# Evictions, operand builds and one held-back product of a three-stage attention and gated-layer kernel: where they stand and which engine runs them

## The chip, the cores and the metric

The kernel runs on one core of a Trainium2 chip. The metric is the device time of one execution in microseconds (us). The profiler times every instruction of one execution. The core has five instruction streams that run beside each other, each in its own order: PE (TensorE, the matrix engine), ACT (ScalarE), DVE (VectorE), POOL (GpSimd) and SP (SyncE), which here issues the DMA transfers.

## The reference

```python
def reference(q, k, v, moe_*, moe2_*):
    # attention: 4 x 8 heads, 576 tokens, head size 64; keys and values averaged over 8 tokens
    attn = softmax(q @ k_p.T / 8) @ v_p            # (4, 8, 576, 64)
    x = attn.transpose(0, 2, 1, 3).reshape(2304, 512)
    # first gated layer, 512 -> 1536 -> 512
    xn = x / sqrt(mean(x * x) + 1e-6) * rms_g
    g = xn @ w_gate
    x = (g * sigmoid(g) * (xn @ w_val)) @ w_out
    # second gated layer, 512 -> 1536 -> 512
    return ((x @ w_a) * (x @ w_b)) @ w_out2        # (2304, 512)
```

The weights of both layers arrive as 64-bit floating point numbers and are converted on the chip.

## The kernel before, in words

**Precision.** Every large matmul is done as three: an operand t is split into a high part (a copy rounded to the type fp32r, made by ScalarE) and a low part (t minus the high part, a subtraction on VectorE or GpSimd). The product is then low x high + high x high + high x low, summed in PSUM, the matrix engine's result memory of 8 banks.

**First layer.** The 2304 tokens are worked off in five tiles of 512, 256, 512, 512 and 512. For each of 12 weight blocks of 128 columns, the loop at the end of the kernel function issues the products g and v (`project`), SiLU, the multiply of both (L1228, VectorE, which frees the PSUM bank of v), the split of the result (L1231, L1232) and, one block later, the output product into four accumulators (`out_proj`). `split_w` (L618) splits the weights of the next block, the low part on GpSimd (L622). After the last block the four accumulators are evicted (L1242): copies 0 and 2 on ScalarE, 1 and 3 on VectorE, into tiles `ev` of the pool `ev_p`, which has two buffers, and stored to DRAM (`x2d`) by SP.

**Second layer.** The tokens are taken in three blocks s of 768, each cut in two halves of tokens and two halves of the 512 features. `w_a` and `w_b` are treated as one 2 x 2 block matrix, and the 2 x 2 block product is computed in Winograd's form with seven block products instead of eight. `build(s, ...)` (L842) prepares the token side: it loads the four quarters, forms the differences t1 to t4 in place (`less`, L874, VectorE) and splits the seven operands b00, b10, t1, b11, t2, t3, t4 (`cast`, L863, ScalarE; `low`, L868: the first feature half on VectorE, the second on GpSimd, two instructions each). It returns eleven steps. `combine` and `convert` do the like for the weight side.

`group(f, s, side)` (L1026) issues six of the seven products of weight block f and token block s, each of six matmuls with 384 columns, into three banks X, Y and Z: X with b00, Y with t1, Z with b10, then further terms on top: X with t2, Y with b11, X with t3. Between them stand copies out of the banks on ScalarE (`snap`, L1023: p1, p5, u2) and additions on VectorE (L1043, L1049, L1054, L1055). After each product one entry of the list `side` is issued (`beside`), and so the build's steps are spread over the groups. The seventh product (t4, on top of X) of a group is held back and issued by `flush` (L1060) in the middle of the next group; it can start only when VectorE's L1054 has read X.

Build 0 runs beside the last tile of the first layer, in `second_front`, one step per quarter of a weight block. Build 1 runs in groups (0, 0) and (1, 0), build 2 in (0, 1) and (1, 1); then come (0, 2), (1, 2) and all others. The pools of the second layer take over the memory of the first's; an instruction that writes into such memory waits until the tile that lay there has been read or stored.

**Output projection.** `out_block` (L1106) adds, for each s, the products of the 12 hidden blocks into six accumulators; `prepare` loads and splits the weights (L1084, L1085) and hidden values (L1093, L1094) of the blocks ahead.

**Order.** In the last tile and the second layer the order of the instructions of PE, ACT, DVE and POOL is that of the program (`manual_schedule`). SP's order is chosen when the kernel is compiled. An engine whose next instruction waits does nothing else.

Of the kernel before, what the change touches and what calls it, by code (L numbers as in the profile page):

```python
# [8 lines left out]
F32 = mybir.dt.float32  # L9
# [8 lines left out]
P = 128  # L18
UNIT = 256
TILES1 = [512, 256, 512, 512, 512]  # L20
SLICE = 768
# [34 lines left out]
def starts(sizes):  # L56
    out, t = [], 0
    for n in sizes:
        out.append((t, n))
        t += n  # L60
    return out
# [3 lines left out]
def attention_moe_moe2(  # L65
# [14 lines left out]
    nc = tc.nc  # L80
# [7 lines left out]
    KD = DM // P  # L88
# [17 lines left out]
    x_p = first.enter_context(tc.tile_pool(name="x", bufs=1))  # L106
    h_p = first.enter_context(tc.tile_pool(name="h", bufs=2))
    ev_p = first.enter_context(tc.tile_pool(name="ev", bufs=2))
# [729 lines left out]
    two = {}  # L838
# [3 lines left out]
    def build(s, new, quarter):  # L842

        part = {}

        def load(h):
            t0 = s * SLICE + h * HALF
            for k in range(2):
                part[h, k] = quarter(f"x_{s}_{h}_{k}")
                for s0, sn in starts(TILES1):  # L850
                    lo, hi = max(s0, t0), min(s0 + sn, t0 + HALF)
                    if lo < hi:
                        for c in range(2):
                            row = (2 * k + c) * P
                            nc.sync.dma_start(
                                out=part[h, k][c][:, lo - t0:hi - t0],
                                in_=x2d[s0][row:row + P, lo - s0:hi - s0],
                            )

        def cast(i, h, k):  # L860
            hi, lo = XC[s, i] = new(s, i)
            for c in range(2):
                nc.scalar.copy(hi[:, c], part[h, k][c])  # L863

        def low(i, h, k):
            hi, lo = XC[s, i]
            for c in range(2):
                (nc.vector if c == 0 else nc.gpsimd).tensor_sub(  # L868
                    lo[:, c], part[h, k][c], hi[:, c].bitcast(F32)
                )  # L870

        def less(dst, a, b):
            for c in range(2):
                nc.vector.tensor_sub(part[dst][c], part[a][c], part[b][c])  # L874

        loads = [lambda: load(0), lambda: load(1)]
        return loads, [
            lambda: (cast("b00", 0, 0), cast("b10", 0, 1)),
            lambda: (low("b00", 0, 0), low("b10", 0, 1)),
            lambda: less((0, 0), (1, 0), (0, 0)),  # L880
            lambda: (cast("t1", 0, 0), cast("b11", 1, 1)),
            lambda: (low("t1", 0, 0), low("b11", 1, 1)),
            lambda: less((0, 0), (1, 1), (0, 0)),
            lambda: (cast("t2", 0, 0), less((1, 0), (1, 1), (1, 0))),
            lambda: (low("t2", 0, 0), cast("t3", 1, 0)),
            lambda: (less((0, 1), (0, 1), (0, 0)), low("t3", 1, 0)),
            lambda: cast("t4", 0, 1),
            lambda: low("t4", 0, 1),
        ]
# [116 lines left out]
    def bank(name):  # L1006
        return two["ps"].tile([P, 512], F32, tag="bank", name=name, bufs=8)

    def product(dst, f, a, s, b, start, stop):
        wh, wl, c0 = WC[f, a]  # L1010
        xh, xl = XC[s, b]
        i = 0
        for c in range(2):
            for w, x in ((wl, xh), (wh, xh), (wh, xl)):
                nc.tensor.matmul(  # L1015
                    dst[:, :HALF], w[:, c0 + c, :], x[:, c, :],
                    start=(start and i == 0), stop=(stop and i == 5), skip_group_check=True,
                )
                i += 1
# [40 lines left out]
    def flush():  # L1060
        if not pending:
            return
        f, s, X, c00 = pending.pop()
        product(X, f, A11, s, "t4", False, True)
        nc.vector.tensor_mul(c00, c00, X[:, :HALF])
        store(f, s, 0, c00)
# [3 lines left out]
    def store(f, s, h, src):  # L1070
        if (f, s) not in hd:
            hd[f, s] = dr.tile([P, SLICE], F32, tag=f"h_{f}_{s}", name=f"h_{f}_{s}")
        nc.sync.dma_start(out=hd[f, s][:, h * HALF:(h + 1) * HALF], in_=src)
# [25 lines left out]
    def prepare():  # L1099
        if todo:  # L1100
            s, f = todo.pop(0)
            if s == 0:
                out_weights(f)
            hidden_of(s, f)

    def out_block(s):  # L1106
        accs = [bank(f"o_{s}_{i}") for i in range(SLICE // P)]

        def add(f, i):
            wh, wl = WO[f]  # L1110
            hh, hl = HO[s, f]
            sub = slice(i * P, (i + 1) * P)
            for j, (x, y) in enumerate(((hh, wl), (hh, wh), (hl, wh))):
                nc.tensor.matmul(  # L1114
                    accs[i], x[:, sub], y, start=(f == 0 and j == 0), stop=(f == NF - 1 and j == 2),
                )

        for f in range(NF - 2):
            for i in range(len(accs)):
                add(f, i)  # L1120
            prepare()
        prepare()
        for i, acc in enumerate(accs):
            for f in range(NF - 2, NF):
                add(f, i)
            ev = two["o"].tile([P, 512], F32, tag="ev2", name=f"ev_{s}_{i}", bufs=3)
            if i % 2 == 0:
                nc.scalar.copy(ev, acc)
            else:
                nc.vector.tensor_copy(ev, acc)  # L1130
            t0 = s * SLICE + i * P
            nc.sync.dma_start(out=out[t0:t0 + P, :], in_=ev)
        prepare()

    later = ctx.enter_context(ExitStack())

    def second_phase():
        def pool(name, **kw):
            return tc.tile_pool(name=name, bufs=1, reuse_waits="tile", **kw)

        two["ps"] = ctx.enter_context(pool("ps2", space=bass.MemoryType.PSUM))
        two["w"] = later.enter_context(pool("w2", side="right"))
        bottom, middle = ctx.enter_context(ExitStack()), ExitStack()
        two["q"] = bottom.enter_context(pool("q2"))
        two["x2"] = bottom.enter_context(pool("x2"))
        two["x1"] = middle.enter_context(pool("x1"))

        def new(s, i):
            return [
                two[f"x{s}"].tile([P, 2, HALF], F32R, tag=f"{i}{e}", name=f"x{e}_{i}_{s}", bufs=1)  # L1150
                for e in "hl"
            ]

        def quarter(name):
            t = two["q"].tile([P, 2, HALF], F32, tag="xq", name=name, bufs=4)
            return [t[:, c] for c in range(2)]

        idle = [lambda: None]
        loads, steps = build(1, new, quarter)
        group(0, 0, loads + idle + steps[:4])  # L1160
        group(1, 0, steps[4:])
        loads, steps = build(2, new, quarter)
        group(0, 1, loads + idle + steps[:4])
        group(1, 1, steps[4:])
        group(0, 2, convert(2, 0) + convert(2, 1))
        group(1, 2, combine(2))
        for f in range(2, NF):
            group(f, 0, convert(f + 1, 0) + convert(f + 1, 1) if f + 1 < NF else convert(NF - 3, 2) + convert(NF - 2, 2))
            group(f, 1, combine(f + 1) if f + 1 < NF else convert(NF - 1, 2))
            if f < NF - 1:  # L1170
                group(f, 2, convert(f - 2, 2))
        middle.close()
        two["o"] = ctx.enter_context(pool("o2"))
        group(NF - 1, 2, idle + [prepare] + idle * 2 + [prepare])
        flush()
        later.close()
        two["r"] = ctx.enter_context(pool("o3", side="right"))
        for s in range(NS2):
            out_block(s)

    last_act = [None]
    for idx, (ph, t0, n) in enumerate(work):
        last_tile = idx + 1 == len(work)
        nxt = None if last_tile else work[idx + 1]
        side = SIDE[idx] if idx < len(SIDE) else []
        region = ExitStack()
        if last_tile:
            attn.close()
            side = second_front()
# [6 lines left out]
        def step():  # L1196
# [6 lines left out]
        accs = first_tile() if idx == 0 else [  # L1203
            ps.tile([P, 512], F32, tag=f"acc{c}", name=f"acc{c}") for c in range(KD)
        ]
# [3 lines left out]
        for f, cols, last, ahead, own in jobs:  # L1209
# [22 lines left out]
            low = nc.vector.tensor_sub(hl[:, :m], ht[:, :m], hh.bitcast(F32)[:, :m])  # L1232
# [7 lines left out]
        if nxt is not None:  # L1240
            xs = split_x(xf_t[idx + 1], nxt[2])
        for c, acc in enumerate(accs):  # L1242
            ev = ev_p.tile([P, 512], F32, tag="ev", name="ev")
            if c % 2 == 0:
                nc.scalar.copy(ev[:, :n], acc[:, :n])
            else:
                nc.vector.tensor_copy(ev[:, :n], acc[:, :n])
            nc.sync.dma_start(out=x2d[t0][c * P:(c + 1) * P, :], in_=ev[:, :n])
        region.close()
    first.close()  # L1250
    with tc.manual_schedule(engines=set(HELD)):
        second_phase()
# [36 lines left out]
```

## Time and profile before

| | |
|---|---|
| three runs | 1046.12, 1047.18, 1047.91 us (median 1047.18) |
| the profiled execution | 1046.91 us, of which the span from the first to the last instruction is 1045.0 |
| PE busy | 978.8 us, 94% of the span |
| DVE, ACT, POOL busy | 63%, 46%, 43% |
| mean granted clock of TensorE | 0.98 of full speed |

Busy shares are means over the whole span; where PE is not busy late in the kernel can be seen in a timeline. In the rows, a line of a timeline gives start, duration, engine, source line, operation and tiles, how many instructions were merged (x2), and in brackets the idle time before it with what ended it. "x<-ev" is a store of an evicted accumulator, "x<-x" a load of a token quarter. The first-layer part ends at about 611 us of the span, the groups at about 890.

### The profile page before, as it was taken

How to read it: one execution, taken by the hardware profiler on the slowest of the kernel's cores; microseconds unless marked ns; L12 is line 12 of the kernel's file. 1: busy time of each engine (PE TensorE's matmuls, PEld its weight loads, DVE VectorE, ACT ScalarE, POOL GpSimd, SP SyncE). 2: the span in 40 equal slices, each digit the busy share in tenths (PEclk: the TensorE clock that was granted, in tenths of full speed). 3: DMA queues.
4: the chain of work that ended last, by engine and by line, in shares of the span. 5: the costliest groups of instructions: out<-in, count | busy, mean ns of one | idle time of the engine just before them, and what ended most of it. 6: DMA issues, size and time to landing. Idle time of an engine off the chain costs nothing.

```text
span 1045.0 us, 13959 instructions
## 1 busy us (share of the span) xinstructions
PE 978.8 (94%) x5044; PEld 858.4 (82%) x5044; DVE 663.0 (63%) x992; ACT 477.0 (46%) x900; POOL 453.0 (43%) x360
## 2 busy tenths in 40 slices
PE   4977899889899999999999988999999998999998
PEld 3766677778788887888788878999999998888886
DVE  6999988996853756363627859766677665322221
ACT  3765764565454536444445435443444434222211
POOL 6476584646543434343359834533334332310000
PEclk9799899999899999999999999999999999999999
DMA  9456534330100002000111133434444444544332
GB/s 231 138 178 192 168 105 123 108 90 2 31 10 21 1 1 61 1 1 1 41 43 60 41 109 99 142 124 152 126 145 143 131 126 170 182 139 136 126 117 74
DMA packets 82804, 101.57 MB, mean 97 GB/s; under 512 B 24112, under 2 KB 63024, under 8 KB 82736
## 3 DMA queue, kind: packets, MB, share of 16 engines
q1 hardware_dynamic: 82736, 100.69, 31.3%
q8 instruction: 40, 0.66, 0.3%
q14 instruction: 28, 0.23, 0.1%
HBM read 73.93 MB, written 26.74 MB: 96 GB/s over the span
## 4 chain that ended last, share of the span: by engine, by line
PE 72%; DVE 18%; issue 3%; DMA 3%; ACT 2%; POOL 1%; SPq 1%; DVEq 0%; ACTq 0%; POOLq 0%
PE o L1114 14%; PE X L1015 13%; PE acc L663 9%; PE g L650 9%; PE v L650 9%; PE Y L1015 6%; PE Z L1015 3%; PE xT L400 2%; PE g L788 2%; DVE wf L600 2%; DVE kp L190 1%; PE sc L319 1%; PE v L788 1%; DVE wf L597 1%; DVE x L874 1%
## 5 line engine op out<-in xcount | busy, mean ns | idle before, releaser
L622 POOL TENSOR_TENSOR wl<-wf,wh 128x512 fp32r<-128x512 f32 x163 | 225.5, 1391 | 226.2 <-ACT wh L621 223.7
L621 ACT CAST wh<-wf 128x512 fp32r<-128x512 f32 x180 | 109.3, 619 | 72.6 <-PE acc L663 32.4
L663 PE MATMUL acc<-hh,wl 128*128 128x512 f32 (+1 forms) x248 | 92.2, 372 | 8.9 <-ACT hh L1231 5.7
L1094 DVE TENSOR_TENSOR hl<-hf,hh 128x768 fp32r<-128x768 f32 x36 | 35.6, 993 | 96.5 <-ACT hh L1093 96.5
L663 PE MATMUL acc<-hl,wh 128*128 128x512 f32 (+1 forms) x248 | 90.2, 368 | 3.6 <-DVE hl L806 3.4
L663 PE MATMUL acc<-hh,wh 128*128 128x512 f32 (+1 forms) x248 | 90.4, 365 | 0.0
L1114 PE MATMUL o<-woh,hl 128*128 128x512 f32 x216 | 86.0, 398 | 0.0
L1114 PE MATMUL o<-woh,hh 128*128 128x512 f32 x216 | 85.3, 395 | 0.0
L1114 PE MATMUL o<-wol,hh 128*128 128x512 f32 x216 | 84.9, 393 | 0.0
L650 PE MATMUL v<-xh,wl 128*128 128x512 f32 (+1 forms) x192 | 72.6, 378 | 2.8 <-DVE ht L1228 2.7
L1093 ACT CAST hh<-hf 128x768 fp32r<-128x768 f32 x36 | 29.8, 834 | 93.6 <-PE o L1114 87.0
L650 PE MATMUL g<-xh,wl 128*128 128x512 f32 (+1 forms) x192 | 71.4, 372 | 0.0
L650 PE MATMUL g<-xl,wh 128*128 128x512 f32 (+1 forms) x192 | 70.8, 369 | 0.1
L650 PE MATMUL g<-xh,wh 128*128 128x512 f32 (+1 forms) x192 | 70.9, 369 | 0.0
L650 PE MATMUL v<-xl,wh 128*128 128x512 f32 (+1 forms) x192 | 69.9, 364 | 0.0
L650 PE MATMUL v<-xh,wh 128*128 128x512 f32 (+1 forms) x192 | 69.6, 363 | 0.0
L607 POOL TENSOR_TENSOR wf<-wf,st 128x512 int32<-128x512 int32 x36 | 52.8, 1467 | 37.2 <-DVE wf L600 17.8
L607 POOL TENSOR_TENSOR w<-w,st 128x512 int32<-128x512 int32 x24 | 31.9, 1331 | 78.5 <-DVE w L600 77.3
L663 PEld LDWEIGHTS acc<-hh,wl 128*128 128x128 f32 x248 | 47.4, 191 | 17.5 <-issue 6.9
L1023 ACT COPY p<-X 128x384 f32<-128x384 f32 x36 | 17.2, 478 | 89.3 <-PE X L1015 89.3
L663 PEld LDWEIGHTS acc<-hl,wh 128*128 128x128 f32 x248 | 46.8, 191 | 12.8 <-DVE hl L806 4.5
L1228 DVE TENSOR_TENSOR ht<-ht,v 128x512 f32<-128x512 f32 (+1 forms) x48 | 29.6, 616 | 42.1 <-PE v L650 40.9
(208 smaller groups left out, 2782.7 us busy)
## 6 DMA issues: line engine op xcount, KB each, us to landing
hf<-h SPq DMA_DIRECT2D x36, 384.0 KB
st<-in_moe_w_out_dram SPq DMA_DIRECT2D x24, 512.0 KB
h<-u SPq DMA_DIRECT2D x36, 192.0 KB
h<-p SPq DMA_DIRECT2D x36, 192.0 KB
st<-in_moe_w_gate_dram SPq DMA_DIRECT2D x12, 512.0 KB
st<-in_moe_w_val_dram SPq DMA_DIRECT2D x12, 512.0 KB
st<-in_moe_w_a_dram SPq DMA_DIRECT2D x12, 512.0 KB
st<-in_moe_w_b_dram SPq DMA_DIRECT2D x12, 512.0 KB
```

The lines of the kernel that those rows point to most:

```text
L400: nc.tensor.matmul(bank[:, off:off + cnt], lhs, rhs, start=(i == 0), stop=(i == len(pairs) - 1),)
L607: nc.gpsimd.tensor_tensor(out=bits, in0=bits, in1=low, op=ALU.add)
L621: nc.scalar.copy(wh, wf[ph, f, i])
L622: (nc.vector if boot["alt"] else nc.gpsimd).tensor_sub(wl, wf[ph, f, i], wh.bitcast(F32))
L650: nc.tensor.matmul(bank[:, :n], w[:, c, :], x[:, c, cols], start=(i == 0), stop=(i == 3 * KD - 1),)
L663: nc.tensor.matmul(accs[c][:, cols], w[:, c, :], x[:, :n], start=(f == 0 and i == 0 and cols.start == 0), stop=(f == NF - 1 and i == 2),)
L788: nc.tensor.matmul(bank[:, :n], w[:, c, :], x[:, c, cols], start=(c == 0 and i == 0), stop=(c == KD - 1 and i == 2),)
L1015: nc.tensor.matmul(dst[:, :HALF], w[:, c0 + c, :], x[:, c, :], start=(start and i == 0), stop=(stop and i == 5), skip_group_check=True,)
L1093: nc.scalar.copy(hh, hf)
L1094: nc.vector.tensor_sub(hl, hf, hh.bitcast(F32))
L1114: nc.tensor.matmul(accs[i], x[:, sub], y, start=(f == 0 and j == 0), stop=(f == NF - 1 and j == 2),)
L1228: nc.vector.tensor_mul(ht[:, :m], ht[:, :m], vb[:, :m])
```

## The change

Three edits are made.
1. In the last tile the four evictions go into the four quarters of one tile of the pool `x_p` (the tag of the tile's input, which is no longer needed) instead of the two `ev` buffers.
2. In `build`, all low parts run on VectorE. The eleven steps are cut anew: one cast of an operand per step where there were up to two, each low part one step later than its cast.
3. The flush after the last group, with the closing of the pools that go with it, moves into the first output block (s = 0), behind the products of hidden block 0 with the first two of the six accumulators. Accumulators are therefore taken one by one, as they are first used.

```diff
@@ -865,9 +865,7 @@
         def low(i, h, k):
             hi, lo = XC[s, i]
             for c in range(2):
-                (nc.vector if c == 0 else nc.gpsimd).tensor_sub(
-                    lo[:, c], part[h, k][c], hi[:, c].bitcast(F32)
-                )
+                nc.vector.tensor_sub(lo[:, c], part[h, k][c], hi[:, c].bitcast(F32))
 
         def less(dst, a, b):
             for c in range(2):
@@ -875,14 +873,14 @@
 
         loads = [lambda: load(0), lambda: load(1)]
         return loads, [
-            lambda: (cast("b00", 0, 0), cast("b10", 0, 1)),
-            lambda: (low("b00", 0, 0), low("b10", 0, 1)),
-            lambda: less((0, 0), (1, 0), (0, 0)),
-            lambda: (cast("t1", 0, 0), cast("b11", 1, 1)),
-            lambda: (low("t1", 0, 0), low("b11", 1, 1)),
-            lambda: less((0, 0), (1, 1), (0, 0)),
+            lambda: cast("b00", 0, 0),
+            lambda: low("b00", 0, 0),
+            lambda: (less((0, 0), (1, 0), (0, 0)), cast("b10", 0, 1)),
+            lambda: (cast("t1", 0, 0), low("b10", 0, 1)),
+            lambda: (cast("b11", 1, 1), low("t1", 0, 0)),
+            lambda: (less((0, 0), (1, 1), (0, 0)), low("b11", 1, 1)),
             lambda: (cast("t2", 0, 0), less((1, 0), (1, 1), (1, 0))),
-            lambda: (low("t2", 0, 0), cast("t3", 1, 0)),
+            lambda: (cast("t3", 1, 0), low("t2", 0, 0)),
             lambda: (less((0, 1), (0, 1), (0, 0)), low("t3", 1, 0)),
             lambda: cast("t4", 0, 1),
             lambda: low("t4", 0, 1),
@@ -1104,9 +1102,11 @@
             hidden_of(s, f)
 
     def out_block(s):
-        accs = [bank(f"o_{s}_{i}") for i in range(SLICE // P)]
+        accs = []
 
         def add(f, i):
+            if f == 0:
+                accs.append(bank(f"o_{s}_{i}"))
             wh, wl = WO[f]
             hh, hl = HO[s, f]
             sub = slice(i * P, (i + 1) * P)
@@ -1115,9 +1115,16 @@
                     accs[i], x[:, sub], y, start=(f == 0 and j == 0), stop=(f == NF - 1 and j == 2),
                 )
 
+        NA = SLICE // P
         for f in range(NF - 2):
-            for i in range(len(accs)):
+            for i in range(NA):
                 add(f, i)
+                if f == 0 and s == 0 and i == 1:
+                    flush()
+                    later.close()
+                    two["r"] = ctx.enter_context(
+                        tc.tile_pool(name="o3", bufs=1, side="right", reuse_waits="tile")
+                    )
             prepare()
         prepare()
         for i, acc in enumerate(accs):
@@ -1172,9 +1179,6 @@
         middle.close()
         two["o"] = ctx.enter_context(pool("o2"))
         group(NF - 1, 2, idle + [prepare] + idle * 2 + [prepare])
-        flush()
-        later.close()
-        two["r"] = ctx.enter_context(pool("o3", side="right"))
         for s in range(NS2):
             out_block(s)
 
@@ -1240,7 +1244,12 @@
         if nxt is not None:
             xs = split_x(xf_t[idx + 1], nxt[2])
         for c, acc in enumerate(accs):
-            ev = ev_p.tile([P, 512], F32, tag="ev", name="ev")
+            if last_tile:
+                if c == 0:
+                    last_x = x_p.tile([P, KD, 512], F32, tag="xf", name="last_x")
+                ev = last_x[:, c]
+            else:
+                ev = ev_p.tile([P, 512], F32, tag="ev", name="ev")
             if c % 2 == 0:
                 nc.scalar.copy(ev[:, :n], acc[:, :n])
             else:
```

## Rows read from the trace of the kernel before

**Rows 1.** The profile's chain that ended last: shares of the span by engine.

```profile
PE 72%; DVE 18%; issue 3%; DMA 3%; ACT 2%; POOL 1%; SPq 1%; DVEq 0%; ACTq 0%; POOLq 0%
```

**Rows 2.** Timeline of PE at the start of the second layer.

```profile
610.75 0.34 PE L1015 MATMUL X<-xh_b,al 128*128 128x384 f32 x1
...
615.39 0.45 PE L1015 MATMUL Z<-xh_b,al 128*128 128x384 f32 x1 [2.39 <-ACT ev L1245]
...
620.34 0.33 PE L1015 MATMUL X<-xh_b,al 128*128 128x384 f32 x1
...
625.05 0.44 PE L1015 MATMUL X<-xh_t,sl 128*128 128x384 f32 x1 [1.43 <-ACT p L1023]
...
642.61 0.44 PE L1015 MATMUL X<-xh_t,sl 128*128 128x384 f32 x1 [1.46 <-ACT p L1023]
...
655.83 0.34 PE L1015 MATMUL X<-xh_b,al 128*128 128x384 f32 x1
...
663.11 0.34 PE L1015 MATMUL X<-xh_b,al 128*128 128x384 f32 x1
```

**Rows 3.** Timeline of ACT in the same stretch.

```profile
614.75 0.58 ACT L1245 COPY ev<-acc 128x512 f32<-128x512 f32 x1 [5.26 <-DMA x<-ev]
...
618.63 0.48 ACT L1023 COPY u<-X 128x384 f32<-128x384 f32 x1 [2.53 <-DMA x<-ev]
...
622.82 0.98 ACT L863 CAST xh_t<-x 128x384 fp32r<-128x384 f32 x2 [2.06 <-DVE x L874]
...
624.53 0.47 ACT L1023 COPY p<-X 128x384 f32<-128x384 f32 x1
```

**Rows 4.** Timeline of SP in the same stretch: issues of transfers.

```profile
607.36 4.61 SPq L855 DMA_DIRECT2D x<-x  x10
...
615.36 1.35 SPq L1248 DMA_DIRECT2D x<-ev  x2
...
634.99 2.38 SPq L855 DMA_DIRECT2D x<-x  x5
```

**Rows 5.** Timelines of PE and DVE where the output projection starts.

```profile
883.60 0.97 DVE L1094 TENSOR_TENSOR hl<-hf,hh 128x768 fp32r<-128x768 f32 x1 [5.17 <-ACT hh L1093]
...
887.22 0.54 DVE L1054 TENSOR_TENSOR p<-p,X 128x384 f32<-128x384 f32 x1
...
884.97 0.34 PE L1015 MATMUL X<-xl_t,rh 128*128 128x384 f32 x1
887.81 0.69 PE L1015 MATMUL X<-xh_t,bl 128*128 128x384 f32 x1 [2.51 <-DVE p L1054]
...
891.82 0.39 PE L1114 MATMUL o<-wol,hh 128*128 128x512 f32 x1
```

**Rows 6.** Windows: stretch, length, busy time (instructions) of each engine, clock, DMA share, GB/s.

```profile
612.00:616.00 4.00, 1.61 (x9) 1.29 (x8) 0.32 (x1) 1.25 (x3) 0.00 (x0) 1.00 0.83 274
...
888.00:891.00 3.00, 3.00 (x9) 2.81 (x10) 1.66 (x3) 0.91 (x2) 0.82 (x2) 0.50 0.89 342
...
900.00:920.00 20.00, 20.00 (x87) 16.08 (x87) 4.27 (x5) 5.80 (x9) 7.70 (x5) 1.00 0.53 154
```

**Rows 7.** VectorE in 607 to 656: groups by line, count, busy us, mean ns.

```profile
L874 DVE TENSOR_TENSOR x<-x,x 128x384 f32<-128x384 f32 x16 | 12.7, 833 | 0.4 <-DMA x<-x 0.4
...
L868 DVE TENSOR_TENSOR xl_b<-x,xh_b 128x384 fp32r<-128x384 f32 x6 | 6.1, 1032 | 0.2 <-ACT xh_b L863 0.2
L868 DVE TENSOR_TENSOR xl_t<-x,xh_t 128x384 fp32r<-128x384 f32 x8 | 6.0, 747 | 0.0
```

**Rows 8.** Timeline of DVE: two subtractions with POOL idle.

```profile
626.78 1.01 DVE L874 TENSOR_TENSOR x<-x,x 128x384 f32<-128x384 f32 x2
```

**Rows 9.** Timelines of DVE and PE in the last tile of the first layer.

```profile
572.76 4.50 DVE L874 TENSOR_TENSOR x<-x,x 128x384 f32<-128x384 f32 x3 [0.91 <-POOL xl_t L868]
...
577.18 0.67 DVE L1228 TENSOR_TENSOR ht<-ht,v 128x512 f32<-128x512 f32 x1
...
578.00 0.47 PE L650 MATMUL v<-xh,wl 128*128 128x512 f32 x1
```

## The prediction

> **What bounds the kernel now.** I read the chain that ended last first: 72% of it is TensorE's, 18% VectorE's [rows 1]. So TensorE sets the time, except where it waits; the next view is therefore the slices, and in them the places where its busy digit falls below 9 late in the kernel, since the change touches only what comes after the last tile of the first layer. Two places are left, and for each I read the timeline, engine by engine.
>
> Place A is the start of the second layer. TensorE starts the first product at 610.75, the group (1, 2), which no longer needs newly built operands, at 655.83, and the next group, without a wait, at 663.11 [rows 2]. A group of seven products thus takes 7.28 us, a product 1.04. Between 610.75 and 655.83 lie 6 + 4 x 7 = 34 products, 35.4 us of work in 45.1 us: 9.7 us are lost, in nine waits, of which the first and the two next in length are shown (idle 2.39, 1.43, 1.46; each also costs some 0.27, in the tail of the matmul before and the slower first one after).
> - The first wait is for the third eviction. Two `ev` buffers serve four evictions, and SP stands in its own queue with ten loads of the next block (607.36 to 611.97) before it stores the first. So ScalarE copies the third accumulator only at 614.75, after 5.26 us idle [rows 3, 4], and product Z, whose bank that accumulator held, starts at 615.39.
> - The `u2` copy then waits until 618.63 for the last stores (issued 615.36 and later): its buffer lies where `ev` lay [rows 3, 4].
> - From there the operand builds are late. ScalarE stands with two casts of `t1` at 622.82, waiting for VectorE's subtraction, casts `b11` too, and only then, at 624.53, copies X of group (1, 0), although X was finished at about 621.5 [rows 2, 3]. TensorE waits for this copy until 625.05; the same happens one build later, at 642.61.
>
> Place B is the passage from the last group to the output projection. The last product of the group starts its sixth matmul at 884.97; the held-back product (`flush`) starts at 887.81, 2.51 us idle, since it writes into the bank that VectorE's L1054 reads at 887.22 [rows 5]. After this wait the granted clock is 0.50, the 1.2 GHz level, from 888 to 891 [rows 6], and the third output block starts at 891.82.
>
> **The change part by part.**
>
> *Evictions.* Removed are two waits for stores; no instruction is added. The copies (0.58 on ScalarE) can follow their accumulators, the last of which is complete as X starts, at 610.75 [rows 2, 3]; the third is out by 611.4 at the latest. X and Y take until 610.75 + 2.08 = 612.83, so Z starts then, without a wait. X/t2 follows at 613.87, Y/b11 at 614.91, X/t3 at 615.95; the `u2` copy is done at 615.6, since its buffer now lies under tiles long out of use. Group (1, 0) starts at 616.99 instead of 620.34: 3.35 us. The other side of it: the new tile's memory goes to the second layer too. By the order of the pools I put it under operands of the next block, of which `b11` is the first due, at 619.4. SP still has 12 loads and 4 stores from 607.36, some 0.46 us each (4.61 for ten), to 614.7; a store has landed 2.8 after SP was free for it (611.97 to 614.75), so 617.4 [rows 3, 4]. Hidden, by 2 us; if an earlier operand lies there, see the third rival.
>
> *Builds.* A build had 14 low parts, 7 on VectorE and 7 on GpSimd, and 8 subtractions. In 607 to 656 VectorE's cost 12.7 + 6.1 + 6.0 = 24.8 us for 16 and 12 to 14 instructions, with means of 747 to 1032 ns [rows 7]. Two of them without a GpSimd instruction beside them take 1.01 [rows 8]; with 0.54 for one, as the add at 887.22 [rows 5], that is 0.47 from start to start. After the change GpSimd has nothing in this stretch, so VectorE does 16 + 28 at 0.47 = 20.7 us: 4 us less, with twice the low parts. Bounds: all at 0.47 (20.7), or all at the 0.83 of before (36.5), which needs a GpSimd at work beside them; its low parts were its only work here, so I take the first and leave the doubt to the first rival.
> The Trainium skill (SBUF — State Buffer, Who interferes with whom) has it that VectorE instructions with two SBUF inputs contend with GpSimd's reads, by a lock that makes the loser wait the whole instruction. The rows agree here; in the last tile, where GpSimd keeps its other splits, the same rule speaks against the change, which is the fourth rival.
>
> With these durations I walked the four engines in program order (product 1.04; a cast or copy on ScalarE some 0.4 from start to start, two casts being 0.98 and one copy 0.48 [rows 3]; VectorE 0.47):
> - Casts of `b00` 615.6 to 616.5; their low parts on VectorE to 617.6; subtraction to 618.6; casts of `b10` meanwhile, of `t1` to 619.1. The copy of X of (1, 0) is done at 619.5, and its reader is due at 620.1. That wait is gone, since `b11`'s casts now stand behind the copy.
> - The second half of the build is paced by VectorE: 22 operand instructions and 10 of two groups, 32 x 0.47 = 15.0 us, against 14.6 us of products. So small waits stay: 0.6 for `u2` of (1, 0), which stands behind the casts of `t2`, and 0.5 for X of (0, 1) behind those of `t4`.
> - Block 2 needs its loads. A slot is free when its last reader is done, by the walk 625.1, 627.4, 628.3 and 630.8. SP's five last loads, at 634.99 before [rows 4], are issued from about 630; with the 2.8 of the store above, rounded up, they land from 633 to 635. This leaves 1.3 us of waits in group (1, 1), and in (0, 2) 1.0 as before, where weights are converted beside it.
> The waits sum to 3.4. The old order, walked in the same way, comes out 0.3 short of the trace, so I take 3.7 for the 9.7: 6.0 us gained.
> Bounds: nothing but the evictions, 3.35; all waits gone, 9.7.
>
> In the last tile the same edit moves seven low parts to VectorE. There TensorE hardly waited; at one place it was close: v at 578.00 starts just when VectorE's L1228 (577.18 and 0.67 long) has freed its bank, behind three subtractions that took 4.50 us beside GpSimd [rows 9]. GpSimd loses seven instructions of about 1.1 there, so fewer of VectorE's are slowed; I take zero.
>
> *Last product.* The flush and what it issues (one VectorE multiply, one store on SP) move behind six output matmuls; the weight and hidden loads behind it on SP are still asked for after it. The low part of the first hidden block, the last of their operands, was done at 884.57 [rows 5]. A matmul of 512 columns takes 20/87 = 0.23 [rows 6], so they fill 885.15 to 886.53. The flush still waits for VectorE until 887.81, as nothing makes that add earlier: a wait of 1.3 stays. At the full clock the flush then takes 1.15, and the third block starts at 888.96 instead of 891.82: 2.9 gained, 1.4 by the work put into the wait and 1.5 by the clock. For the clock: a wait of 2.39 at 613 left it at 1.00, where this one of 2.51 ended at 0.50 [rows 2, 6]; one of 1.3 is well under both. If it falls still, 1.4 remain. Bounds: 0, if VectorE's add moves later by as much; 4.2, if it comes earlier by the whole wait.
>
> Sum: 6.0 + 2.9 = 8.9. The profiled execution took 1046.91 (span 1045.0, 1.9 around it), so 1038.0; the median is 0.27 above it, so 1038.3.
>
> **The rivals.**
> 1. *The builds stay late.* VectorE alone carries all low parts, and block 2's loads land 3 us later than I have it; the walk then loses 3 more, A gives 3.0, and the time is 1041.3. For: VectorE at 15.0 against 14.6 has no slack. Against: it is less loaded than before.
> 2. *The last product gains nothing*, because the output matmuls fill only a wait whose end VectorE sets and the clock falls again: at most 1.4, so 1039.8 to 1041.2. For: VectorE's add is untouched. Against: the shorter wait.
> 3. *The wait for the stores only moves* (the change doesn't do what it says): the tile lies under an operand or copy needed at once. If X's first copy waits until 617.4, X/t2 slips from 613.87 to 617.9, by 4.0: 1042.3; if `b00`'s cast does, by 1.8: 1040.1.
> 4. *Slower: VectorE fails in the last tile.* Its multiply frees the bank of v, and at 577.85 was just in time [rows 9]. Seven more low parts beside GpSimd's splits at 4.50/3 = 1.5 each would cost 10.5 us, and two waits long enough for the 0.50 clock (1.5 each) 3 more: 13.5 against 8.9 gained, 1051.8. It decides from a loss of 8.9 on, six of the seven slowed and uncovered. The lock of the skill's page is this mechanism. Against it: GpSimd's own load there falls.
>
> **How the numbers follow.** Forecast 0.58, with a range of its own from 1036.5 to 1040; first rival 0.18, second 0.09, third 0.09, fourth 0.06. A measurement of this kernel tells 0.2%, 2.1 us, from no change. Forecast and rivals 1 to 3 are beyond it on the fast side, except for mixes of the three (1045 and up), which have 0.05 of their 0.36; of the fourth, 0.04 lies over 2.1 us slower and 0.02 below. So faster 0.89, same 0.07, slower 0.04. The range reaches from 1035.5 (half of the waits that I leave in A are gone as well, or the add comes earlier) to 1043.0, past the first three rivals; outside are the fourth, the mixes and the tails.
>
> **What would show it.** After: third eviction before 612; Z right behind Y; no GpSimd instruction of L868; subtractions near 0.5; (1, 0) starting 6.2 us after the first product instead of 9.6, (1, 2) 39 us after it instead of 45.1; clock 1.00 through the passage to the output projection, and the flush between second and third output block with a wait near 1.3. The prediction is wrong if TensorE shows new waits between 560 and 610, if ScalarE waits for a store in the first group, or if a wait of over 2 us stands in groups (0, 1) or (1, 1).

## The result and the profile after

The changed kernel takes 1035.36 us (median of 5 runs, 1034.97 to 1036.3) against 1047.18 for the kernel before (5 runs, 1044.2 to 1049.0): a ratio of 0.989, 95% interval 0.9871 to 0.9908, that is 11.8 us less. The forecast was 1038.3 with a range down to 1035.5; the gain is 2.9 us larger than forecast, and the time lies 0.1 us under the range.

Both profiled executions, cut at the same instructions of TensorE, give the account. The stretches follow each other, so that they sum to the span.

| stretch on TensorE | before | after | gain | forecast |
|---|---|---|---|---|
| start to the first product of the last tile | 512.49 | 510.90 | 1.59 | 0 (no edit there) |
| last tile, 12 weight blocks | 98.26 | 97.93 | 0.33 | 0 |
| first product of the second layer to group (1, 2) | 45.08 | 38.05 | 7.03 | 6.0 |
| group (1, 2) to the last X/t3, sixth matmul | 229.14 | 229.34 | -0.20 | 0 |
| from there to the third output block | 6.85 | 3.83 | 3.02 | 2.9 |
| the rest, to the end of the span | 153.15 | 153.15 | 0 | 0 |

The three stretches with a gain that an edit touches hold 10.4 us, 10.2 after the 0.2 given back; the 95% interval of the gain, 9.6 to 13.5 us, holds this as well. The 1.59 lies ahead of all code that an edit touches: among the fourteen profiles of this study the last tile starts between 510.38 and 512.76, with an edited kernel at either end (the last section shows one reason). Whether it is chance alone is taken up with the prediction.

The chain that ended last is as before [rows 1], two hundredths more of it TensorE's:

```profile
PE 74%; DVE 18%; issue 3%; DMA 2%; ACT 2%; POOL 1%; SPq 0%; ACTq 0%; DVEq 0%
```

The timeline of TensorE at the start of the second layer, against [rows 2]: first product, Z, group (1, 0), in brackets the first two of the four waits that the trace shows (the others, 0.25 and 0.17, follow in group (0, 2)), groups (1, 2) and (2, 0).

```profile
608.83 0.34 PE L1013 MATMUL X<-xh_b,al 128*128 128x384 f32 x1
...
610.91 0.33 PE L1013 MATMUL Z<-xh_b,al 128*128 128x384 f32 x1
...
615.07 0.33 PE L1013 MATMUL X<-xh_b,al 128*128 128x384 f32 x1
...
626.25 0.45 PE L1013 MATMUL X<-xh_t,sl 128*128 128x384 f32 x1 [0.19 <-ACT p L1021]
...
637.46 0.44 PE L1013 MATMUL X<-xh_t,rl 128*128 128x384 f32 x1 [0.31 <-ACT u L1021]
...
646.88 0.34 PE L1013 MATMUL X<-xh_b,al 128*128 128x384 f32 x1
...
654.25 0.34 PE L1013 MATMUL X<-xh_b,al 128*128 128x384 f32 x1
```

Z starts 2.08 us after X, right behind Y, and (1, 0) comes 6.24 us after the first product, where it was 9.59. ScalarE, against [rows 3]: the third eviction is done 0.1 us after X starts (608.92) and well ahead of Z, `u2` waits for X alone, and the copy of X of group (1, 0), at 617.17, ends 0.55 us before the matmul that needs it (618.19).

```profile
608.34 0.58 ACT L1254 COPY last_x<-acc 128x512 f32<-128x512 f32 x1 [0.77 <-PE acc L663]
...
613.19 0.48 ACT L1021 COPY u<-X 128x384 f32<-128x384 f32 x1 [1.60 <-PE X L1013]
...
616.28 0.98 ACT L863 CAST xh_t<-x 128x384 fp32r<-128x384 f32 x2 [0.96 <-DVE x L872]
617.17 0.47 ACT L1021 COPY p<-X 128x384 f32<-128x384 f32 x1
```

SP, against [rows 4]: ten loads, then the four stores without a pause; the last four loads of block 2 go out at 628.17, 19.3 us after the first product, where the last five went out 24.2 after it.

```profile
604.56 4.62 SPq L855 DMA_DIRECT2D x<-x  x10
609.28 2.14 SPq L1257 DMA_DIRECT2D x<-last_x  x4
...
628.17 1.82 SPq L855 DMA_DIRECT2D x<-x  x4
```

VectorE's groups in 608 to 656, against [rows 7]: 16 subtractions and 28 low parts take 22.5 us, where 16 and 14 took 24.8; each takes 551 ns, where the means were 747 to 1032.

```profile
L872 DVE TENSOR_TENSOR x<-x,x 128x384 f32<-128x384 f32 x16 | 8.2, 552 | 0.6 <-DMA x<-x 0.6
L868 DVE TENSOR_TENSOR xl_t<-x,xh_t 128x384 fp32r<-128x384 f32 x16 | 8.2, 551 | 0.0
L868 DVE TENSOR_TENSOR xl_b<-x,xh_b 128x384 fp32r<-128x384 f32 x12 | 6.1, 551 | 0.0
```

Where the output projection starts, against [rows 5], first TensorE, then VectorE. The flush (878.89) waits 0.93 instead of 2.51, and the third output block starts at 880.05.

```profile
876.22 0.34 PE L1013 MATMUL X<-xl_t,rh 128*128 128x384 f32 x1
...
878.89 0.45 PE L1013 MATMUL X<-xh_t,bl 128*128 128x384 f32 x1 [0.93 <-DVE p L1052]
...
880.05 0.39 PE L1114 MATMUL o<-wol,hh 128*128 128x512 f32 x1
```

```profile
876.78 1.13 DVE L1092 TENSOR_TENSOR hl<-hf,hh 128x768 fp32r<-128x768 f32 x1
...
878.29 0.54 DVE L1052 TENSOR_TENSOR p<-p,X 128x384 f32<-128x384 f32 x1
```

The window behind it, against [rows 6], has the clock at 1.00 where it was 0.50:

```profile
879.00:882.00 3.00, 3.00 (x15) 2.66 (x16) 2.33 (x3) 0.85 (x2) 0.49 (x1) 1.00 1.02 324
```

In the last tile, against [rows 9], VectorE's multiply is done at 574.6 and v starts at 576.18: 1.6 us of slack where there was none. VectorE's row first, TensorE's behind it.

```profile
573.92 0.67 DVE L1232 TENSOR_TENSOR ht<-ht,v 128x512 f32<-128x512 f32 x1
```

```profile
576.18 0.39 PE L650 MATMUL v<-xh,wl 128*128 128x512 f32 x1
```

### The profile page after: what moved, and what is told of

It reads as the page before. It is cut to its first block, busy times and chain, and to the rows that moved or that the text cites. A ratio compares the mean times of both kernels' runs of the same rounds, so it can differ in the third digit from the quotient of the medians.

```text
span 1033.2 us, 13954 instructions
## 1 busy us (share of the span) xinstructions
PE 976.8 (95%) x5044; PEld 857.9 (83%) x5044; DVE 659.0 (64%) x1013; ACT 477.2 (46%) x900; POOL 428.3 (41%) x339
## 4 chain that ended last, share of the span: by engine, by line
PE 74%; DVE 18%; issue 3%; DMA 2%; ACT 2%; POOL 1%; SPq 0%; ACTq 0%; DVEq 0%
PE o L1114 14%; PE X L1013 13%; PE v L650 10%; PE acc L663 9%; PE g L650 9%; PE Y L1013 6%; PE Z L1013 3%; PE xT L400 2%; DVE wf L600 2%; DVE wf L597 1%; PE sc L319 1%; PE g L788 1%; DVE hl L806 1%; PE eT L368 1%; DVE kp L190 1%
```

## The experiments

The theory after the result: three separate gains that add, the evictions, the builds (by their order more than by their engine), and the last product. The rivals: the evictions are the whole gain at the start of the second layer; GpSimd beside VectorE, not the order, made the builds late; the low clock at the flush is luck of an execution. The stretches (us) and times of all runs; "to (1, 0)" and "to (1, 2)" count from the first product, "flush" from the sixth matmul of the last X/t3 to the third output block.

| kernel | to (1, 0) | to (1, 2) | last tile | flush | time, median (runs) |
|---|---|---|---|---|---|
| before | 9.59 | 45.08 | 98.26 | 6.85 | 1047.18 (5) |
| e0: before again | 9.58 | 44.85 | 98.25 | 6.53 | 1046.96 (1) |
| changed | 6.24 | 38.05 | 97.93 | 3.83 | 1035.36 (5) |
| e12: changed again | 6.24 | 38.75 | 97.93 | 3.80 | 1034.61 (4) |
| e1: evictions alone | 6.24 | 42.01 | 98.26 | 7.29 | 1043.66 (8) |
| e2: builds alone | 8.98 | 39.68 | 97.93 | 7.24 | 1041.15 (4) |
| e3: last product alone | 9.66 | 44.92 | 98.20 | 3.80 | 1042.85 (10) |
| e4: changed, low parts half on GpSimd | 6.25 | 42.25 | 99.05 | 3.82 | 1040.95 (1) |
| e5: changed, old step order | 6.25 | 37.72 | 97.92 | 3.83 | 1034.54 (1) |
| e6: changed, second preparation late | 6.25 | 38.32 | 97.92 | 2.65 | 1035.48 (1) |
| e7: changed, flush behind four blocks | 6.24 | 38.10 | 97.93 | - | 1035.64 (1) |
| e9: changed, idle GpSimd work added | 6.24 | 42.68 | 97.93 | 3.81 | 1041.25 (1) |
| e10: the combination | 6.25 | 37.71 | 97.92 | 2.98 | 1033.57 (4) |
| e11: before, second preparation late | 9.85 | 45.30 | 98.21 | 4.05 | 1043.14 (1) |

### The kernel before, again

No edit.

> The kernel before, unchanged, profiled a second time, to see which differences belong to the change and which to the single execution. Stretches in the first profile: first product to group (1, 2) 45.08 us; sixth matmul of the last X/t3 to the third output block 6.85 us; twelve blocks of the last tile 98.26 us; last tile starts at 512.49 us. Theory: 45.08 and 98.26 come back within 0.3; the clock of 0.50 behind the flush's wait comes back too, so 6.85 stays. Rival (the clock after a wait of 2.5 us is a matter of the single execution): this stretch comes out near 5.4 at full clock; likewise the start of the last tile moves by up to 1.6, because the 1.4 us that the first profile lost at 242 to 246 us at a low clock are not lost again.

The stretches come back within 0.32, and so does the low clock behind the flush: windows behind that wait (idle 2.31 here) show 0.50 again.

```profile
888.00:891.00 3.00, 2.96 (x9) 2.77 (x10) 1.29 (x3) 0.79 (x2) 0.29 (x2) 0.50 0.89 266
```

### Each edit alone

e1 has the eviction hunk of the diff alone, e2 the two hunks in `build`, e3 the hunks of `out_block` and `second_phase`.

> Edit 1 alone: last tile evicts into one free tile, builds and flush as before. Theory (three separate gains that add): first product to (1, 0) 6.24 instead of 9.59; first product to (1, 2) about 41.7 instead of 45.08, since the build waits of about 1.7 each come back; flush stretch 6.85; time 3.4 us below the kernel before. Rival A (the evictions are the whole of place A, the builds only looked late because ScalarE started late): first product to (1, 2) near 38, time 7 us below.

> Edit 2 alone: single casts, low parts on VectorE, evictions and flush as before. Theory: first product to (1, 0) stays 9.6; first product to (1, 2) about 41.5 to 42.7 instead of 45.08; the last tile's v at the eighth block no longer waits for VectorE, twelve blocks in 97.9; flush stretch 6.85; time 3 us below the kernel before. Rival A: (1, 2) at 45, time the same. Rival B (VectorE overloaded in the last tile): twelve blocks longer than 98.3.

> Edit 3 alone: flush behind the first two output blocks, rest as before. Theory: sixth matmul of X/t3 to the third output block 3.8 instead of 6.85, with a wait near 1 us and the clock at 1.00; first product to (1, 2) stays 45.1; time 3.0 us below the kernel before. Rival (the gain at this place needs the earlier landing of loads that the other edits bring): 5 or more. Rival (clock is luck): time only 1.4 below, as the kernel before then has the low clock in only some of its executions.

e1: (1, 0) at 6.24 as expected, (1, 2) at 42.01, so 3.07 us gained there; ratio 0.9964, interval 0.9951 to 0.9977. The evictions are not the whole. At the flush its clock stayed low longer, from 882 to 888, which cost 0.4 to the third output block and more behind it:

```profile
882.00:888.00 6.00, 5.54 (x15) 4.77 (x16) 3.13 (x4) 1.45 (x2) 2.90 (x2) 0.50 0.93 306
```

e2: (1, 2) at 39.68, 5.4 us gained, although 1.84 of the first wait's 2.39 us is still there; that is 1.8 to 3.0 more than expected. Ratio 0.9947 (0.9931 to 0.9964). No rival holds; the theory had the size wrong. Its wait at the flush was the longest of all, and the low clock came behind it here too:

```profile
881.26 0.44 PE L1013 MATMUL X<-xh_t,bl 128*128 128x384 f32 x1 [3.02 <-DVE p L1052]
```

```profile
882.00:885.00 3.00, 3.00 (x10) 2.54 (x9) 1.42 (x2) 0.80 (x2) 1.37 (x1) 0.53 0.92 303
```

e3: 3.80 at the flush, clock 1.00, nothing else moved; ratio 0.9964 (0.9953 to 0.9975). Edit 3 is independent of the others.

Edits 1 and 2 overlap: 3.07 and 5.40 alone, 7.03 together, 1.4 less than the sum. That with both the builds are paced by a VectorE without pauses and by block 2's loads is argued from the timeline, not shown.

### Order or engine

```diff
# e4 (of the changed kernel): every second low part back on GpSimd
-                nc.vector.tensor_sub(lo[:, c], part[h, k][c], hi[:, c].bitcast(F32))
+                (nc.vector if c == 0 else nc.gpsimd).tensor_sub(
+                    lo[:, c], part[h, k][c], hi[:, c].bitcast(F32)
+                )
# e5 (of the changed kernel): the eleven steps of the kernel before
-            lambda: cast("b00", 0, 0),
-            lambda: low("b00", 0, 0),
...
+            lambda: (cast("b00", 0, 0), cast("b10", 0, 1)),
+            lambda: (low("b00", 0, 0), low("b10", 0, 1)),
...
```

> The changed kernel, but every second low part back on GpSimd: the new order of the eleven steps with the old engines. The changed kernel has 38.05 us from the first product to group (1, 2) and 97.93 for the twelve blocks of the last tile; with both parts of the old build (edit 1 alone) it was 42.01 and 98.26. Theory (order first: the copies of X no longer stand behind casts that wait for VectorE): 37.5 to 39, last tile 98.2. Rival (GpSimd beside VectorE is what made the builds late): 41 or more.

> The changed kernel with the old eleven steps (two operands cast per step), all low parts on VectorE: the new engine with the old order. Theory (order first): ScalarE still casts b11 ahead of the copy of X, so waits of near 1 us stay at the second group of each build: 39.5 to 41 from the first product to group (1, 2). Rival (contention alone): 38.0, as in the changed kernel. Twelve blocks of the last tile 97.9 by both, if it is GpSimd's low parts that held VectorE up there.

The theory falls, the rival stands. With the new order and GpSimd still in it, (1, 2) is at 42.25, no better than e1's 42.01, and the last tile is even 0.8 longer than before. With the old order and all on VectorE it is at 37.72 (37.71 in e10, whose build is the same), where the four profiles with the build of the change lie between 38.05 and 38.75: the new order gains nothing and may cost some tenths. First e4: two waits of TensorE, and VectorE's groups.

```profile
625.25 0.44 PE L1015 MATMUL X<-xh_t,rl 128*128 128x384 f32 x1 [1.14 <-ACT u L1023]
...
630.28 0.44 PE L1015 MATMUL X<-xh_t,sl 128*128 128x384 f32 x1 [0.57 <-ACT p L1023]
```

```profile
L874 DVE TENSOR_TENSOR x<-x,x 128x384 f32<-128x384 f32 x16 | 12.3, 806 | 0.7 <-DMA x<-x 0.6
...
L868 DVE TENSOR_TENSOR xl_b<-x,xh_b 128x384 fp32r<-128x384 f32 x6 | 6.4, 1065 | 0.0
L868 DVE TENSOR_TENSOR xl_t<-x,xh_t 128x384 fp32r<-128x384 f32 x8 | 6.0, 751 | 0.0
```

The new order does shorten the wait that it was made for, since the wait of 1.73 that e1 has for the copy of X is 0.44 here, but with VectorE as slow as before the time is only lost one step later, at `u2`. In e5 the old order's waits are there (1.10 and 0.44 for the copy of X, the first shown), and the products behind them run without one:

```profile
619.46 0.44 PE L1013 MATMUL X<-xh_t,sl 128*128 128x384 f32 x1 [1.10 <-ACT p L1021]
```

### GpSimd work that nobody waits for

```diff
                 nc.vector.tensor_sub(lo[:, c], part[h, k][c], hi[:, c].bitcast(F32))
+                if c == 1 and s > 0:
+                    scr = two["x1"].tile([P, HALF], F32, tag="scr", ...)
+                    high = hi[:, c].bitcast(F32)
+                    nc.gpsimd.tensor_sub(scr, high, high)
```

> The changed kernel, plus 14 GpSimd subtractions of 128x384 in builds 1 and 2, each issued when the second high part of an operand is cast, into a scratch tile that nobody reads: the old GpSimd load without anything that waits for its results. The changed kernel has VectorE means of 551 ns at its low parts and subtractions, and 38.05 us from the first product to group (1, 2). Theory (VectorE and GpSimd slow each other): means of 650 to 850 ns, since each GpSimd instruction holds up about one of VectorE's, and 42 or more to group (1, 2), as 14 times some 0.7 us are added to a VectorE that has no slack. Rival (the old builds were late because the subtractions waited for GpSimd's results, 1.0 to 1.3 us each): means stay at 551 and 38.05 stays.

VectorE's and GpSimd's groups in 608 to 656:

```profile
L868 DVE TENSOR_TENSOR xl_b<-x,xh_b 128x384 fp32r<-128x384 f32 x12 | 10.7, 928 | 0.0
L876 DVE TENSOR_TENSOR x<-x,x 128x384 f32<-128x384 f32 x16 | 8.8, 589 | 0.0
L868 DVE TENSOR_TENSOR xl_t<-x,xh_t 128x384 fp32r<-128x384 f32 x16 | 8.1, 548 | 0.0
...
L872 POOL TENSOR_TENSOR scr_t<-xh_t 128x384 f32<-128x384 f32 x8 | 7.7, 965 | 16.9 <-ACT xh_t L863 16.9
L872 POOL TENSOR_TENSOR scr_b<-xh_b 128x384 f32<-128x384 f32 x6 | 5.4, 905 | 12.2 <-ACT xh_b L863 11.8
```

VectorE's 44 instructions take 27.6 us instead of 22.5, and (1, 2) slips from 38.05 (38.75 when run again) to 42.68. So the presence of GpSimd's instructions is enough; no wait of any engine in this stretch ends with one of them. The Trainium skill (SBUF — State Buffer, Who interferes with whom) says that of the two the loser waits for the whole instruction of the other. The trace agrees: the first of VectorE's pairs below meets a GpSimd instruction in each half and takes 2.28 us, its end standing 0.42 behind the end of GpSimd's second (622.79 against 622.37); the second pair meets none and takes 1.02.

```profile
620.22 1.05 POOL L872 TENSOR_TENSOR scr_t<-xh_t 128x384 f32<-128x384 f32 x1 [2.04 <-ACT xh_t L863]
621.42 0.95 POOL L872 TENSOR_TENSOR scr_b<-xh_b 128x384 f32<-128x384 f32 x1
...
620.51 2.28 DVE L868 TENSOR_TENSOR xl_b<-x,xh_b 128x384 fp32r<-128x384 f32 x2
622.71 1.02 DVE L868 TENSOR_TENSOR xl_t<-x,xh_t 128x384 fp32r<-128x384 f32 x2
```

In all, 14 instructions of 0.94 us cost VectorE 5.1 us, 0.36 each: of VectorE's 44, the 18 that overlap one take 838 ns in the mean, and the 26 that meet none 548.

### The last wait

```diff
# e6, e11: second preparation behind the last addition of the last group
-        group(NF - 1, 2, idle + [prepare] + idle * 2 + [prepare])
+        group(NF - 1, 2, idle + [prepare] + idle * 4 + [prepare])
# e7: flush behind four output blocks
-                if f == 0 and s == 0 and i == 1:
+                if f == 0 and s == 0 and i == 3:
# e10: evictions and flush of the change, all low parts on VectorE, old step order, and
+        group(NF - 1, 2, idle * 3 + [prepare] + idle * 2 + [prepare])
```

> The changed kernel, with the second preparation of the output projection (weights and hidden values of block 1) issued after the last addition of the last group instead of ahead of it. Theory (the flush's remaining wait of 0.93 is for VectorE's addition, which stands behind the low part of hidden block 1, and that behind a load): the wait is gone, sixth matmul of X/t3 to the third output block 2.8 instead of 3.83, to the first matmul with hidden block 1 5.4 instead of 6.58; end 1.1 us earlier. Rival (the addition itself is late because X is): the wait stays. Other rival: the low part is now too late for hidden block 1, and the wait reappears there, 6.5.

> The changed kernel, with the flush behind four output blocks instead of two: 12 matmuls of 0.23, 2.8 us, fill more than the 2.3 that passed from X/t3 to the flush. Theory: no wait at the flush, first matmul with hidden block 1 at 5.4 instead of 6.58 after the sixth of X/t3; end 1.1 us earlier. Rival (a later flush delays VectorE's multiply and through it the low part of hidden block 2 and the loads behind the store): a new wait at hidden block 2 or 3, end the same.

> The kernel before with one step moved: the second preparation of the output projection behind the last addition of the last group; the flush stays where it was. Theory (the flush waited for an addition that stood behind the low part of hidden block 1, and the low clock came from that wait): wait at the flush under 1 us instead of 2.51, clock 1.00 behind it, sixth matmul of X/t3 to the third output block 3.4 instead of 6.85. Rival (the low clock belongs to the passage to other operands): 0.50 stays and the stretch is 4.5 or more.

e6: no wait at the flush, 2.65 to the third output block and 5.41 to hidden block 1 (6.58 in the changed kernel). VectorE's addition did stand behind the low part. Some of it was lost ahead of X/t3, where `u2` waited 0.87 instead of 0.50 behind casts that wait for a load.

e7: half a miss. Hidden block 1 starts at 6.13, a gain of 0.45 and not 1.1, as a wait of 0.50 stays. The load of hidden block 1 came later in this run, its low part ran at 878.98 and the addition at 880.32, 0.9 us later against X/t3 than in the changed kernel. Whether the edit had a part in the late load is not shown by this one run. A filled wait is worth only as much as its end stays put. First TensorE, then VectorE:

```profile
880.93 0.44 PE L1013 MATMUL X<-xh_t,bl 128*128 128x384 f32 x1 [0.50 <-DVE p L1052]
```

```profile
878.98 0.96 DVE L1092 TENSOR_TENSOR hl<-hf,hh 128x768 fp32r<-128x768 f32 x1 [1.12 <-ACT hh L1091]
...
880.32 0.55 DVE L1052 TENSOR_TENSOR p<-p,X 128x384 f32<-128x384 f32 x1
```

e11: the kernel before needs no move of the flush for most of this gain. The wait falls to 1.17, the clock stays at 1.00, and the stretch is 4.05 instead of 6.85 (3.4 expected; VectorE's two additions, 0.55 long each and 0.46 from start to start, still follow X/t3, so about a microsecond remains). So the low clock goes with the long wait.

```profile
885.42 0.44 PE L1015 MATMUL X<-xh_t,bl 128*128 128x384 f32 x1 [1.17 <-DVE p L1054]
```

```profile
885.00:889.00 4.00, 3.58 (x17) 3.15 (x18) 3.73 (x5) 1.46 (x2) 1.73 (x1) 1.00 0.98 315
```

### A combination

> The version that the runs point to: edits 1 and 3, all low parts on VectorE, the old eleven steps, and both preparations of the output projection later in the last group, behind the copy u2 and behind the last addition. Theory: first product to group (1, 2) 37.7; last group to its sixth matmul of X/t3 7.5 instead of 8.0, since ScalarE's copy u2 no longer stands behind casts that wait for loads; from there to hidden block 1 5.4 instead of 6.58; together 1.9 us below the changed kernel, about 1033.5. Rival (the loads of the output projection set this passage, not the order): a new wait at hidden block 0 or 1, time as the changed kernel or up to 1 us above.

> The changed kernel, unchanged, on the same chip and in the same rounds as the version that combines (both theories the same): 1035.4, 38.05 to group (1, 2), 3.83 at the flush.

e10 takes 1033.57 (1033.13 to 1033.79; ratio to the kernel before 0.9868, 0.9852 to 0.9885), e12 1034.61 (1032.79 to 1037.03; 0.9881, 0.9861 to 0.9901). e10 beats the kernel before by 13.4 us; against the changed kernel the intervals overlap, so the times alone don't tell them apart. The stretches that it edits are shorter in its profile by 1.9 us: from the first product to (2, 0) 45.13 against 45.42, from the start of the last group to its sixth matmul of X/t3 7.24 against 7.99, on to hidden block 1 5.73 against 6.58 (5.4 expected). The first of these differences, 0.3, is less than that between the changed kernel's own two profiles (45.42 and 46.15).

## Why the prediction was right or wrong

**The evictions** were sized right: 3.35 us to group (1, 0), forecast and measured. The other side of the edit, the stores under the next block's operands, cost nothing: SP has issued them by 611.4, and the casts of `b11` that may wait for them start at 617.54, without a wait.

**The builds** were right in the price of an instruction (0.47 from start to start), but the "4 us less" for VectorE set 20.7 us counted from start to start against 24.8 of busy time; busy time alone falls from 24.8 to 22.5, by 2.3. And the explanation had one wrong step. "That wait is gone, since `b11`'s casts now stand behind the copy" put part of the gain down to the order. e4 and e5 show that the order gains nothing here, alone or with the rest, and that taking GpSimd's low parts away gains all of it; in e5 the wait that was credited to the order is still there, 1.10 us, and (1, 2) comes no later for it. So the term came near in part by luck. The mistake was to count the one long wait that goes, and not to ask what the engine behind it, VectorE, could then deliver. The term was 6.0 and is 7.03 in the first profile; with all profiles of either kind of build (44.85 to 45.30 before, 38.05 to 38.75 after) it is between 6.1 and 7.3. The mis-sized part are the waits that were left in: 3.7 forecast, 38.05 - 35.4 = 2.7 measured.

**The last tile** was taken at zero and gave 0.33. The fourth rival had the sign of the danger wrong there: seven more low parts did not make VectorE late, because GpSimd's own went, and the multiply now has 1.6 us of slack. Where GpSimd keeps them (e4), the new order makes the tile 0.8 us longer than before, and TensorE waits 0.85 for VectorE's multiply at 577.82. The fourth rival's mechanism is real, then, but the change works against it.

**The last product** was right: 2.9 forecast, 3.02 measured, with a remaining wait of 0.93 (1.3 forecast) and the clock at 1.00. That the wait's end is set by VectorE's addition behind the low part of hidden block 1 is shown by e6 and e11.

**The rest** of the difference, 1.6 us between the two profiles, was not in the forecast and lies in no stretch that an edit touches: with the other small terms the edits account for 10.2 of the 11.8. It may be more than the luck of two profiles. From the start of the last tile to the end, the profiles of e1, e2 and e3 gain 2.0, 4.8 and 3.1 us, but their medians lie 3.6, 6.1 and 4.4 under the 1047.23 of the kernel before (17 runs beside theirs), so that 1.3 to 1.6 is left over each time. The cause stays open. The first, second and third rivals did not happen: `b00`'s casts start right behind `u2` at 613.57, no copy waits for a store, and no wait of over 0.31 us is left in the builds.

## What to carry to other kernels

When two engines can share elementwise work, price it with both running: 14 instructions put beside VectorE cost more time than they took off it, and moving them all to VectorE made it faster in sum. A reordering that removes the longest wait in a list may only hand the time to the next one; test it apart from what else changes. A wait before a matmul can have a second price in the clock, so look at the granted clock behind each wait, and at what the producer of the awaited value stood behind, before filling the wait with other work.

## What the runs showed of the hardware that was not expected

The low clock at the flush was no luck: in all four profiles with a wait of 2.31 to 3.02 us at that place (before, e0, e1, e2) the granted clock fell to 0.50, the 1.2 GHz level, for between 3 and 7 us. In the profiles with 1.17 or less it did not. But a wait of about the same length at the start of the second layer (2.39 to 2.68 in before, e0, e3, e11) never lowered it. TensorE had worked without a pause ahead of that one, while at the flush a wait of 0.4 to 1.0 for `u2` came a microsecond earlier. What decides is not settled by these runs.

A third place, at 242 us in code that no edit touches, goes either way: of fourteen profiles four show the low clock there (before, e0, e3, e9), behind a wait of 2.3 us that all have. The other ten show it at 213 instead, for as long (3.4 us), behind a wait of 3.1 that all have too. So a wait of the same length lowers the clock in one execution and not in another. The stretch at 242 costs about 1.4 us, most of the 1.6 by which the two main profiles differ ahead of the last tile: the matmuls behind its wait start at 241.87 in the kernel before and 241.99 in the changed one, the next of their kind with 64 columns of weights at 253.44 and 252.18. Both profiles of the kernel before show it there and two of the twelve of edited kernels, too few to tell whether that is chance. At 242 the kernel before, then the changed kernel, and the same at 213:

```profile
242.00:245.00 3.00, 3.00 (x17) 3.00 (x18) 1.43 (x4) 1.47 (x4) 2.23 (x2) 0.58 0.02 5
```

```profile
242.00:245.00 3.00, 3.00 (x26) 3.00 (x27) 1.95 (x6) 2.25 (x6) 2.23 (x2) 1.00 0.02 5
```

```profile
213.00:217.00 4.00, 3.70 (x31) 3.70 (x32) 4.00 (x7) 3.06 (x8) 2.76 (x3) 1.00 0.00 0
```

```profile
213.00:217.00 4.00, 3.78 (x19) 3.78 (x20) 4.00 (x7) 1.94 (x5) 2.36 (x2) 0.57 0.00 0
```
